# Threshold attention and a GELU MLP on one core: tail scores in two quarters of the array, joint transposes, and sums made earlier

## The chip, the cores and the metric

The kernel runs on one NeuronCore of a Trainium2 chip. Five engines work side by side, each through its own instructions in order, and wait for each other by semaphores: TensorE (PE in the profile, with PEld for the loads of its stationary operand), VectorE (DVE), ScalarE (ACT), GpSimd (POOL) and SyncE (SP, which here only issues transfers). Transfers between HBM and the on-chip memory (SBUF) are issued by SP, ACT and POOL and run on 16 DMA engines. PE writes its results into PSUM banks, from which DVE and ACT read.

The metric is the device time of one execution in microseconds (us). Ten runs of the kernel before gave a median of 1429.69 us, from 1428.52 to 1432.79.

## The reference

Inputs are `q`, `k`, `v` of shape (8 batches, 8 heads, 576, 64) in float32, a scalar `tau`, and two weights in float64, `w_in` (512 x 2048) and `w_out` (2048 x 512). For each head:

```
scores = q @ k.T / 8
scores = where(scores >= max(scores) - tau, scores, -1e9)      # per row
attn   = exp(scores - max(scores));  attn = attn / (sum(attn) + 1e-9)
out    = attn @ v
```

The heads are laid side by side into `x` (4608 tokens x 512), and the result is `gelu(x @ w_in) @ w_out` with the exact (erf) GELU, again 4608 x 512.

## The kernel before

**Attention.** Two heads, A and B (`e` = 0 and 1 in the code), are handled together as a pair: 64 channels each, so that the two fill 128 partitions. There are 32 pairs. The 576 queries of a pair are cut into four chunks of 128 (main slots, i = 0 to 3) and a rest of 64 (the tail slot, i = 4 = `NC`). The Python loop at the end of the kernel goes over the 160 slots `n` = (pair p, chunk i) and writes out, slot by slot, the order of instructions of each engine; nothing reorders them later.

In a slot, `scores` (L346) multiplies queries by keys. The 576 keys are done in two halves `h` of 288. In a main slot head A has its 64 channels in rows 0 to 63 of the array and head B in rows 64 to 127: four matmuls, each with 64 rows and 128 columns, into two PSUM tiles, one for each head. In a tail slot, both heads have 64 queries each. `q_tail` is a 128 x 128 tile that holds A's tail queries in its upper left and B's in its lower right quarter and zeros elsewhere (memsets on POOL, L102). Two matmuls over the whole array put A's scores into PSUM partitions 0 to 63 and B's into 64 to 127 of one tile. PSUM tiles of the tag `sc` have two buffers, taken in turn. In the profile each float32 matmul is two records.

`softmax_head` (L358) takes the negated row maximum on DVE (L367), the threshold on POOL (L368) and the exponential on ACT (L370). `softmax_tail` (L373) multiplies by the threshold's mask and sums, on DVE (L386); this is the last reader of the PSUM tile. For pairs 4 and later `turn_p` (L423) transposes the weights in 32 x 32 blocks on DVE, one operation for each head, B first, into `pd[0]` and `pd[1]` (or `pd_tail`), and `regroup` (L435) moves the blocks into place by transfers on SP, eight for two main slots. `weigh_v` (L450) multiplies by `v` two slots into the next pair, with matmuls of 128 rows and 64 columns, and DVE divides by the sums (L478), which have gone through HBM and back (`divisors`, L402).

The first four pairs (`EARLY`) are done in another way: PE transposes q, k (L275, L283) and the weights (L301, against a diagonal of the divisors made by ACT, L400, after a reciprocal on DVE, L397).

**Weights.** The float64 weights come in 32 pieces of 128 x 512, by two transfers each on POOL's queue (L154, L156), and are turned into float32 by bit operations: DVE (L176, L183, L185, L187) and ACT (L177). `conversions` is a generator; `convert(ns)` in the slot loop lets it advance by about `ns` of DVE time in each slot: 3000 in slots 0 to 7, 3650 after that, and all the rest at slot 19. Each finished piece calls `load_piece` for another. Odd pieces land in `pd`.

**MLP.** Blocks of 256 tokens. Blocks 0 to 9 go through two plain layers, L520 and L532, whose matmuls `fill` puts between the attention's, by a schedule of goals (`GOAL`, `PARTS`) in the slot loop. Blocks 10 to 17 are done after the attention, two at a time in four duos, by `strassen` (L607): seven products in place of eight on quarters of the operands. Its operands need sums: of `w_in` (`weights_in`, L581, called in the slot after the last attention slot, 12 operations; and L612 inside `strassen`), of the tokens (`x_sums`, L649, once for each duo) and of `w_out` (L658). Blocks 10 to 12 wait in HBM (`put_away`, `bring`) for lack of room. Results leave by rows of 512 (L537, L744, L749).

**Tables.** Exp and GELU need different tables in ACT; `table` (L504) reloads Exp's after each GELU by a small activation on the tile `warm`.

Of the kernel before, what the change touches and what calls it, by code (L numbers as in the profile page):

```python
# [18 lines left out]
def kernel(  # L19
# [69 lines left out]

    ident = const.tile([P, P], FP32, name="ident")  # L90
# [3 lines left out]
    q_tail = [const.tile([P, P], FP32, name=f"q_tail{i}") for i in range(4)]  # L94
    v_sb = [const.tile([P, 2, KR, D], FP32, name=f"v{i}") for i in range(4)]
    pd = [const.tile([P, 4 * KR, P], FP32, name=f"pd{e}") for e in range(2)]
# [4 lines left out]
    for t in q_tail + v_sb:  # L101
        nc.gpsimd.memset(t, 0.0)  # L102
# [156 lines left out]
    def turn_qk_early(p):  # L259
# [26 lines left out]
        for e in range(2):  # L286
            rows = slice(e * D, (e + 1) * D)
            nc.scalar.activation(
                qt[rows, e * TAIL:(e + 1) * TAIL], tr[rows, 0, 0:TAIL], AF.Copy, bias=0.0, scale=q_scale[rows])
# [36 lines left out]
    def turn_qk(p):  # L326

        s = st[p]
        qT = s["qT"] = ld.tile([P, MAIN], FP32, tag="qT", name="qT")
        kT = s["kT"] = ld.tile([P, S], FP32, tag="kT", name="kT")
        qt = s["q_tail"] = q_tail[p % 4]
        qs, ks = s.pop("q"), s.pop("k")
        nc.vector.transpose(kT.rearrange("p (b i) -> p b i", i=Q), ks)
        nc.scalar.activation(qs, qs, AF.Copy, bias=0.0, scale=q_scale)
        nc.vector.transpose(
            qT.rearrange("p (c a i) -> p c a i", c=NC, i=Q),
            qs[:, 0:MAIN // Q, :].rearrange("p (a c) j -> p c a j", c=NC))  # L340
        for e in range(2):
            rows = slice(e * D, (e + 1) * D)
            nc.vector.transpose(
                qt[rows, e * TAIL:(e + 1) * TAIL].rearrange("p (b i) -> p b i", i=Q), qs[rows, MAIN // Q:NB, :])

    def scores(p, i):  # L346
        s = st[p]
        n = 1 if i == NC else 2
        sc = s["sc", i] = [ps.tile([P, 2, 512], FP32, tag="sc", name="sc", bufs=2) for _ in range(n)]
        for h in range(2):  # L350
            for e in range(n):
                rows = slice(0, P) if i == NC else slice(e * D, (e + 1) * D)
                lhsT = s["q_tail"] if i == NC else s["qT"][rows, i * P:(i + 1) * P]
                at = h * HALF + (TAIL if p < EARLY and e == 0 else 0)
                nc.tensor.matmul(  # L355
                    sc[e][:, h, 0:HALF], lhsT=lhsT, rhs=s["kT"][rows, at:at + HALF], start=True, stop=True)
# [66 lines left out]
    def turn_p(p, i):  # L423
# [6 lines left out]
        n = 1 if i == NC else 2  # L430
        for e in reversed(range(n)):
            to = pd_tail[p % 2] if i == NC else pd[e][:, :, i * Q:(i + 1) * Q]
            nc.vector.transpose(to[:, 0:NB, :], w[:, e * S:(e + 1) * S].rearrange("p (b i) -> p b i", i=Q))  # L433
# [58 lines left out]
    warm = const.tile([P, 2], FP32, name="warm")  # L492
    nc.vector.memset(warm, 0.0)

# [15 lines left out]
    def block_steps(n):  # L510

        g = {}
        for j in range(N_DF):
# [11 lines left out]
        for m in range(TOK // P):  # L525
            for j in range(N_DF):
                yield NS_OUT, len(pieces) - N_DF + j + 1
# [11 lines left out]
    mlp = {"n": 0, "steps": None, "next": None, "debt": 0.0}  # L539
# [41 lines left out]
    def weights_in():  # L581
# [3 lines left out]
        rest = [units(v_sb[i % 4])[0] for i in range(NP - 4, NP - 1)]  # L585
# [9 lines left out]
        return (s1, s2, s4), room + rest  # L595
# [11 lines left out]
    def strassen(ext, room):  # L607
        s1, s2, s4 = ext
        for h in range(HF // U):
            for c in range(NK):  # L610
                a = w_in_sb[c][:, HF + h * U:HF + (h + 1) * U]
                vec.tensor_tensor(a, w_in_sb[c][:, h * U:(h + 1) * U], a, op=ALU.subtract)  # L612
        room = room + units(v_sb[(NP - 1) % 4]) + [u for t in pd_tail for u in units(t)]
        room += [x for _ in range(2) for x in unit(xg, "x", 2)]
        x_ext = [room.pop().rearrange("p (c t) -> p c t", c=NK) for _ in range(3)]
# [33 lines left out]
        def x_sums(n1, n2):  # L649
            t1, t2, t4 = x_ext  # L650
            a, b = x_blk[n1], x_blk[n2]
            b11, b21, b12, b22 = a[:, 0:NK, :], a[:, NK:2 * NK, :], b[:, 0:NK, :], b[:, NK:2 * NK, :]
            vec.tensor_tensor(t1, b12, b11, op=ALU.subtract)
            vec.tensor_tensor(t2, b22, t1, op=ALU.subtract)
            vec.tensor_tensor(b12, b22, b12, op=ALU.subtract)  # L655
            vec.tensor_tensor(t4, b21, t2, op=ALU.subtract)

# [7 lines left out]

        def finish_chunk(j, x, p3):
# [6 lines left out]
        x_sums(*DUOS[0])  # L673
        for sb, (n1, n2) in enumerate(DUOS):
# [45 lines left out]
            for m in ms:  # L720
# [3 lines left out]
                vec.tensor_tensor(lo[m][:, 0:HD], lo[m][:, 0:HD], vs[m], op=ALU.add)  # L724
            for n in DUOS[sb + 1] if sb + 1 < len(DUOS) else ():
                if n in away:
                    bring(n)
            if sb + 1 < len(DUOS):
                x_sums(*DUOS[sb + 1])
# [7 lines left out]
            for m in ms:  # L737
                product(ys[m], rows(g22, m, wt4))
                vec.tensor_tensor(hi[m][:, 0:HD], hi[m][:, 0:HD], ys[m], op=ALU.add)
            for m in ms:  # L740
                product(xs[m], rows(gs1, m, wt1))
                vec.tensor_tensor(hi[m][:, HD:2 * HD], hi[m][:, HD:2 * HD], xs[m], op=ALU.add)
                row = n2 * TOK + m * P
                nc.sync.dma_start(out[row:row + P, :], hi[m])  # L744
            for m in ms:
                product(xs[m], rows(g12, m, w_out_part(1, 1)))
                nc.scalar.copy(lo[m][:, HD:2 * HD], xs[m])
                row = n1 * TOK + m * P
                nc.sync.dma_start(out[row:row + P, :], lo[m])  # L749

    load_early(0)
    load_early(1)
# [32 lines left out]
    for n in range(len(slots) + WEIGH + 1):  # L785
# [60 lines left out]
        convert(3000 if n < 2 * HP else 3650 if n < BATCH - 1 else 1e9)  # L846
# [54 lines left out]
```

## Time and profile before

| | |
|---|---|
| Median of ten runs | 1429.69 us |
| The profiled execution | 1430.06 us, span 1427.9 us from its first to its last instruction |
| Granted TensorE clock, mean | 0.995 |
| Main-slot scores, L355 64\*128 64x288 | x960, 165.8 us busy, mean 435 ns |
| Tail-slot scores, L355 128\*128 128x288 | x120, 34.3 us busy, mean 408 ns |
| Transposes of the weights, L433 | x224 into `pd`, 160.7 us busy, mean 756 ns |
| Transposes of tail queries, L343 | x56, 12.2 us busy, mean 218 ns |
| HBM | 71.68 MB read, 11.47 MB written |

How to read the profile: a form such as 64\*128 64x288 gives the rows and columns of the array that a matmul uses and the shape of its moving operand. Matmuls are pipelined, so that the lengths of consecutive records overlap; the distance between two starts is what counts. "Idle before" is the time an engine stood still ahead of an instruction, with what ended it. The slices of the page cut the span into 40 parts of 35.7 us and give the busy share in tenths. All line numbers are those of the kernel before.

### The profile page before, as it was taken

How to read it: one execution, taken by the hardware profiler on the slowest of the kernel's cores; microseconds unless marked ns; L12 is line 12 of the kernel's file. 1: busy time of each engine (PE TensorE's matmuls, PEld its weight loads, DVE VectorE, ACT ScalarE, POOL GpSimd, SP SyncE). 2: the span in 40 equal slices, each digit the busy share in tenths (PEclk: the TensorE clock that was granted, in tenths of full speed). 3: DMA queues.
4: the chain of work that ended last, by engine and by line, in shares of the span. 5: the costliest groups of instructions: out<-in, count | busy, mean ns of one | idle time of the engine just before them, and what ended most of it. 6: DMA issues, size and time to landing. Idle time of an engine off the chain costs nothing.

```text
span 1427.9 us, 19776 instructions
## 1 busy us (share of the span) xinstructions
PE 1381.5 (97%) x6544; PEld 959.4 (67%) x6544; DVE 899.5 (63%) x1908; ACT 640.4 (45%) x1039; POOL 387.7 (27%) x810
## 2 busy tenths in 40 slices
PE   6898899999999999999999999999999999999999
PEld 4676447466465574655746657466488888888887
DVE  5887787877767777777777777777654142241330
ACT  5768525446255373562735627457142141230320
POOL 4443244443434434434334344330000000000000
PEclk9999999999999999999999999999999999999999
DMA  9978167776667776677766777765500100100000
GB/s 267 289 266 241 47 143 151 151 147 130 133 140 144 156 142 140 137 143 158 159 134 144 161 156 149 142 134 99 107 0 1 45 1 0 59 1 8 22 1 30
DMA packets 449492, 167.06 MB, mean 117 GB/s; under 512 B 413040, under 2 KB 432048, under 8 KB 449392
## 3 DMA queue, kind: packets, MB, share of 16 engines
q1 hardware_dynamic: 423184, 108.65, 39.1%
q0 software_dynamic: 23808, 56.57, 12.8%
q8 instruction: 53, 0.87, 0.3%
q10 hardware_dynamic: 2400, 0.59, 0.2%
q14 instruction: 47, 0.39, 0.1%
HBM read 71.68 MB, written 11.47 MB: 58 GB/s over the span
## 4 chain that ended last, share of the span: by engine, by line
PE 85%; DVE 6%; ACT 5%; DMA 2%; issue 1%; POOL 0%; SPq 0%; DVEq 0%; ACTq 0%; POOLq 0%
PE bank L641 27%; PE hT L520 18%; PE o_ps L532 18%; PE sc L355 12%; PE xT L460 10%; ACT p L370 2%; DVE p L386 2%; DVE nmx L367 1%; DMA raw<-in_moe_w_in_dram 1%; DVE power L185 1%; ACT L500 1%; PE tr L301 1%; ACT diag L400 1%; DMA pd<-in_moe_w_in_dram 1%; ACT L507 0%
## 5 line engine op out<-in xcount | busy, mean ns | idle before, releaser
L370 ACT ACTIVATE p<-sc,nmx 128x576 f32<-128x576 f32 x288 | 202.4, 739 | 384.1 <-DVE nmx L367 384.0
L367 DVE TENSOR_REDUCE nmx<-sc 128x1 f32<-128x576 f32 x288 | 204.8, 748 | 148.3 <-PE sc L355 148.3
L520 PE MATMUL hT<-x,w_in 128*128 128x256 f32 x1280 | 296.2, 384 | 0.0
L532 PE MATMUL o_ps<-w_out,g 128*128 128x512 f32 x640 | 294.2, 602 | 0.0
L520 PEld LDWEIGHTS hT<-x,w_in 128*128 128x128 f32 x1280 | 238.4, 190 | 56.9 <-issue 25.2
L386 DVE SCALAR_TENSOR_TENSOR p<-sc,thr,p 128x576 f32<-128x576 f32 x288 | 225.3, 816 | 65.5 <-ACT p L370 64.4
L368 POOL TENSOR_SCALAR thr<-nmx,tau_eff 128x1 f32<-128x1 f32 x288 | 84.6, 294 | 547.0 <-DVE nmx L367 544.5
L532 PEld LDWEIGHTS o_ps<-w_out,g 128*128 128x128 f32 x640 | 116.6, 190 | 140.3 <-issue 138.7
L355 PE MATMUL sc<-kT,qT 64*128 64x288 f32 x960 | 165.8, 435 | 2.6 <-DVE p L386 2.3
L460 PE MATMUL xT<-pT,v 128*64 128x288 f32 (+2 forms) x1280 | 164.1, 409 | 3.2 <-ACT g L500 3.2
L433 DVE STREAM_TRANSPOSE pd<-p 128x576 f32<-128x576 f32 x224 | 160.7, 756 | 2.9
L355 PEld LDWEIGHTS sc<-kT,qT 64*128 64x128 f32 x960 | 93.6, 188 | 84.3 <-issue 71.8
L460 PEld LDWEIGHTS xT<-pT,v 128*64 128x64 f32 x1280 | 90.6, 137 | 72.6 <-issue 13.2
L232 POOL DMA_DIRECT2D v<-in_v_dram x208 | 110.6, 534 | 10.4 <-issue 9.4
L641 PE MATMUL bank<-x,w_in 128*128 128x256 f32 x384 | 94.8, 383 | 3.2 <-DVE x L655 3.2
L507 ACT ACT_TABLE_LOAD x71 | 91.1, 1283 | 1.3
L500 ACT ACT_TABLE_LOAD x71 | 91.1, 1283 | 1.2
L641 PE MATMUL bank<-unit 128*128 128x256 f32 x352 | 88.6, 382 | 0.0
L641 PEld LDWEIGHTS bank<-x,w_in 128*128 128x128 f32 x384 | 73.7, 192 | 14.2 <-issue 4.1
L223 POOL DMA_DIRECT2D q<-in_q_dram x104 | 70.7, 685 | 15.6 <-issue 14.8
L301 PE MATMUL tr<-diag,p 128*128 128x128 f32 (+1 forms) x360 | 49.8, 302 | 25.0 <-ACT diag L400 16.0
L641 PEld LDWEIGHTS bank<-unit 128*128 128x128 f32 x352 | 67.5, 192 | 9.4
(143 smaller groups left out, 1342.1 us busy)
## 6 DMA issues: line engine op xcount, KB each, us to landing
pT<-pd SPq DMA_DIRECT2D x448, 160.0 KB, 3.9
pT<-pd_tail SPq DMA_DIRECT2D x112, 80.0 KB, 2.9
q<-in_q_dram POOLq DMA_DIRECT2D x104, 72.0 KB, 3.9
k<-in_k_dram POOLq DMA_DIRECT2D x104, 72.0 KB, 2.6
out_dram<-o_sb SPq DMA_DIRECT2D x28, 256.0 KB, 3.9
inv<-turned SPq DMA_DIRECT2D x56, 128.0 KB, 3.9
v<-in_v_dram POOLq DMA_DIRECT2D x156, 40.0 KB, 3.0
raw<-in_moe_w_in_dram POOLq DMA_DIRECT2D x8, 512.0 KB, 6.7
```

The lines of the kernel that those rows point to most:

```text
L232: eng.dma_start(t[r:P:4, e, 0:n, :], rows[:, r * KR:r * KR + n, :])
L355: nc.tensor.matmul(sc[e][:, h, 0:HALF], lhsT=lhsT, rhs=s["kT"][rows, at:at + HALF], start=True, stop=True)
L367: nc.vector.tensor_reduce(nmx[:, e:e + 1], sc, axis=AXIS.XY, op=ALU.max, negate=True)
L370: nc.scalar.activation(w[:, e * S:(e + 1) * S].rearrange("p (h s) -> p h s", h=2), sc, AF.Exp, bias=nmx[:, e:e + 1], scale=1.0)
L386: nc.vector.scalar_tensor_tensor(row, sc[e][:, :, 0:HALF], thr[:, e:e + 1], row, op0=ALU.is_ge, op1=ALU.mult, accum_out=den[e])
L433: nc.vector.transpose(to[:, 0:NB, :], w[:, e * S:(e + 1) * S].rearrange("p (b i) -> p b i", i=Q))
L460: nc.tensor.matmul(xT[f, 0:hi - lo], lhsT=s["v"][:, e, c, :], rhs=pT[:, c, lo:hi], start=(c == 0), stop=(c == KR - 1))
L500: nc.scalar.activation(t, hT, AF.Gelu)
L507: nc.scalar.activation(warm[:, 1:2], warm[:, 0:1], AF.Exp)
L520: nc.tensor.matmul(hT[:, j % 2, :], lhsT=w_in_sb[c][:, j * P:(j + 1) * P], rhs=x_blk[n][:, c, :], start=(c == 0), stop=(c == N_DM - 1))
L532: nc.tensor.matmul(o[:, 0:d_model], lhsT=g[j][:, m * P:(m + 1) * P], rhs=w_out_sb[j], start=(j == 0), stop=(j == N_DF - 1))
L641: nc.tensor.matmul(to, lhsT=l, rhs=r, start=start and k == 0, stop=k == len(pairs) - 1, skip_group_check=not start)
```

## The change

1. `q_tail` becomes 128 x 64: the queries of A in partitions 0 to 63, those of B in 64 to 127, without zeros and their memsets. The scores of a tail slot are four matmuls of 64 rows and 64 columns. Head A uses the upper left quarter of the array and head B the lower right one; while A does one half of the keys, B does the other, so that the two write different PSUM banks.
2. `q_tail` is filled by one operation in place of two (ACT in the early pairs, DVE in the others).
3. The two tiles `pd` become views of one tile, and `turn_p` transposes both heads by one operation.
4. The four updates of `w_in` (L612) and the first `x_sums` move from `strassen` into `weights_in`; their room comes from the tiles of `v`.
5. Strassen's results are stored by half rows, each half when it is done. One of these stores stands ahead of `bring` in SP's order.
6. The `warm` tile is set first, and Exp's table is loaded right after the first pair's loads are issued.
7. Conversions: `convert` advances by 0 in slot 0 and by 3400 in slots 1 to 7.

```diff
+    warm = const.tile([P, 2], FP32, name="warm")
+    nc.vector.memset(warm, 0.0)
...
-    q_tail = [const.tile([P, P], FP32, name=f"q_tail{i}") for i in range(4)]
+    q_tail = [const.tile([P, TAIL], FP32, name=f"q_tail{i}") for i in range(4)]
-    pd = [const.tile([P, 4 * KR, P], FP32, name=f"pd{e}") for e in range(2)]
+    turned_p = const.tile([P, 2, 4 * KR, P], FP32, name="turned_p")
+    pd = [turned_p[:, e, :, :] for e in range(2)]
-    for t in q_tail + v_sb:
+    for t in v_sb:
         nc.gpsimd.memset(t, 0.0)
...
+        nc.scalar.activation(qt, tr[:, 0, 0:TAIL], AF.Copy, bias=0.0, scale=q_scale)
...
+        nc.vector.transpose(qt.rearrange("p (b i) -> p b i", i=Q), qs[:, MAIN // Q:NB, :])
...
-        for h in range(2):
-            for e in range(n):
-                rows = slice(0, P) if i == NC else slice(e * D, (e + 1) * D)
-                lhsT = s["q_tail"] if i == NC else s["qT"][rows, i * P:(i + 1) * P]
-                at = h * HALF + (TAIL if p < EARLY and e == 0 else 0)
-                nc.tensor.matmul(
-                    sc[e][:, h, 0:HALF], lhsT=lhsT, rhs=s["kT"][rows, at:at + HALF], start=True, stop=True)
+        for k in range(2):
+            for e in range(2):
+                rows = slice(e * D, (e + 1) * D)
+                if i == NC:
+                    h = (k + e) % 2
+                    to, lhsT = sc[0][rows, h, 0:HALF], s["q_tail"][rows]
+                else:
+                    h = k
+                    to, lhsT = sc[e][:, h, 0:HALF], s["qT"][rows, i * P:(i + 1) * P]
+                at = h * HALF + (TAIL if p < EARLY and (e == 0 or i == NC) else 0)
+                nc.tensor.matmul(to, lhsT=lhsT, rhs=s["kT"][rows, at:at + HALF], start=True, stop=True)
...
-        for e in reversed(range(n)):
-            to = pd_tail[p % 2] if i == NC else pd[e][:, :, i * Q:(i + 1) * Q]
-            nc.vector.transpose(to[:, 0:NB, :], w[:, e * S:(e + 1) * S].rearrange("p (b i) -> p b i", i=Q))
+        if i == NC:
+            nc.vector.transpose(pd_tail[p % 2][:, 0:NB, :], w[:, 0:S].rearrange("p (b i) -> p b i", i=Q))
+            return
+        nc.vector.transpose(
+            turned_p[:, :, 0:NB, i * Q:(i + 1) * Q], w.rearrange("p (e b i) -> p e b i", e=2, i=Q))
...
-        rest = [units(v_sb[i % 4])[0] for i in range(NP - 4, NP - 1)]
+        x_ext = [units(v_sb[i % 4])[0].rearrange("p (c t) -> p c t", c=NK) for i in range(NP - 4, NP - 1)]
...
+        for h in range(HF // U):
+            for c in range(NK):
+                a = w_in_sb[c][:, HF + h * U:HF + (h + 1) * U]
+                vec.tensor_tensor(a, w_in_sb[c][:, h * U:(h + 1) * U], a, op=ALU.subtract)
+        x_sums(x_ext, *DUOS[0])
...
+        def store(n, m, t, at):
+            row = n * TOK + m * P
+            nc.sync.dma_start(out[row:row + P, at:at + HD], t[:, at:at + HD])
...
                 vec.tensor_tensor(lo[m][:, 0:HD], lo[m][:, 0:HD], vs[m], op=ALU.add)
+                store(n1, m, lo[m], 0)
...
     load_early(0)
+    nc.scalar.activation(warm[:, 1:2], warm[:, 0:1], AF.Exp)
     load_early(1)
...
-        convert(3000 if n < 2 * HP else 3650 if n < BATCH - 1 else 1e9)
+        convert(0 if n == 0 else 3400 if n < 2 * HP else 3650 if n < BATCH - 1 else 1e9)
```

## The prediction

> **What bounds the kernel now.** I read the page's busy table and slices first, then the timeline of PE around score slots, then the junction near 1030 us, then the first 40 us.
>
> ```profile
> PE 1381.5 (97%) x6544; PEld 959.4 (67%) x6544; DVE 899.5 (63%) x1908; ACT 640.4 (45%) x1039; POOL 387.7 (27%) x810
> PE   6898899999999999999999999999999999999999
> ```
>
> PE is busy 97% of the span. By windows it is busy 133.8 us of the first 166, 837.4 of the 843 us from 166 to 1009, 20.8 of the 24 us to 1033, and 389.5 of the last 395. So the first 166 us are bound by a chain through DVE, ACT and transfers; after that, whatever PE must do more is paid, and what other engines save is worth nothing unless PE waits for it.
>
> The timeline of PE (start, length, form, count, idle before) shows what score slots cost. A main slot is eight records in row halves (64\*128), a tail slot four records over the whole array (128\*128).
>
> ```profile
> 268.23 2.84 PE L532 MATMUL o_ps<-w_out,g 128*128 128x512 f32 x6
> 271.00 1.24 PE L355 MATMUL sc<-kT,qT 64*128 64x288 f32 x8
> 272.17 4.56 PE L532 MATMUL o_ps<-w_out,g 128*128 128x512 f32 x10
> 276.56 1.13 PE L355 MATMUL sc<-kT,q_tail 128*128 128x288 f32 x4
> 277.53 1.88 PE L532 MATMUL o_ps<-w_out,g 128*128 128x512 f32 x4
> 279.34 0.75 PE L355 MATMUL sc<-kT,qT 64*128 64x288 f32 x2
> 280.34 1.21 PE L355 MATMUL sc<-kT,qT 64*128 64x288 f32 x6 [0.25 <-DVE p L386]
> ```
>
> Starts count, since lengths overlap. The tail slot takes 277.53 - 276.56 = 0.97 us: 4 x 0.242, nothing lost at either side. A main slot streams the same 0.97 (eight records, two at once), but takes 1.17 from its start to the next product, and the products beside it lose time too: the x6 group takes 2.77 where six records 0.429 apart take 2.57. Record by record, an undisturbed main slot holds PE for 1.37 us, 0.40 more than a tail slot: 0.09 on entering the tiled form, 0.10 before its second pair, 0.10 on leaving, 0.10 before the second product after it. The value products, tiled by columns, show the same:
>
> ```profile
> 539.18 5.07 PE L460 MATMUL xT<-pT,v 128*64 128x288 f32 x40
> 544.18 2.84 PE L532 MATMUL o_ps<-w_out,g 128*128 128x512 f32 x6
> ```
>
> Twenty pairs at 0.242 are 4.85; they take 5.00. With entry and re-entry 0.09 + 0.05 + 0.10 + 0.10 = 0.34; here only 0.05 is lost before the second pair, for weight loads of 64 columns take 137 ns against 190.
>
> After each tail slot stands a wait. The next main slot's second matmul must take over the tail's PSUM buffer, held until DVE has finished with it:
>
> ```profile
> 277.74 0.76 DVE L367 TENSOR_REDUCE nmx<-sc 128x1 f32<-128x576 f32 x1 [0.79 <-PE sc L355]
> 279.37 0.82 DVE L386 SCALAR_TENSOR_TENSOR p<-sc,thr,p 128x576 f32<-128x576 f32 x1 [0.88 <-ACT p L370]
> ```
>
> So 279.34 starts with one head and its partner comes at 280.34. Against 1.37 us, the 27 main slots that follow a tail slot from 166 us on lose 0.52 us (14 of them), 0.87 to 1.66 (7) and 0.10 (6).
>
> The junction to the Strassen stage, and the start:
>
> ```profile
> 1028.12 1.03 PE L641 MATMUL bank<-x,w_in 128*128 128x256 f32 x4
> 1032.39 2.04 PE L641 MATMUL bank<-x,w_in 128*128 128x256 f32 x4 [3.24 <-DVE x L655]
> ```
>
> ```profile
> 1026.96 0.95 DVE L478 TENSOR_TENSOR x<-xT,inv 128x64 f32<-128x64 f32 x4 [5.05 <-DMA inv<-turned]
> 1027.83 2.48 DVE L612 TENSOR_TENSOR w_in<-w_in 128x512 f32<-128x512 f32 x4
> 1031.56 0.68 DVE L655 TENSOR_TENSOR x<-x 128x512 f32<-128x512 f32 x1
> ```
>
> ```profile
> 14.31 0.42 DVE L176 TENSOR_SCALAR expo<-raw 128x512 uint32<-128x512 uint32 x1
> ...
> 19.79 0.43 DVE L176 TENSOR_SCALAR expo<-raw 128x512 uint32<-128x512 uint32 x1 [2.00 <-DMA raw<-in_moe_w_in_dram]
> ...
> 20.54 1.40 DVE L367 TENSOR_REDUCE nmx<-sc 128x1 f32<-128x576 f32 x2
> 21.32 3.90 PE L301 MATMUL tr<-diag,p 128*128 128x128 f32 x20 [4.52 <-ACT diag L400]
> 24.76 0.61 POOL L154 DMA_DIRECT2D raw<-in_moe_w_in_dram  x1
> ...
> 33.87 0.43 DVE L176 TENSOR_SCALAR expo<-pd 128x512 uint32<-128x512 uint32 x1 [1.33 <-DMA pd<-in_moe_w_in_dram]
> ```
>
> **The change, part by part** (against the profiled execution, 1430.06 us: span 1427.9 and 2.2 around it; it stands 0.4 above the median, 1429.69).
>
> *Tail scores, steady part.* 28 slots from 166 us on. Four matmuls of 64x64 replace two of 128x128: eight records in pairs stream the same 0.97. No row shows quarters. Bounds: nothing (if they enter and leave like 128\*128), and 0.40 (row halves). I take 0.34, the column form, since quarters also load 64 columns: 28 x 0.34 = +9.6. Part comes back. The last score of the tail ends 0.14 later (entry 0.09, second pair 0.05), the next main slot starts 0.34 later, so its wait for the tail's buffer shrinks by 0.20: 21 x 0.20 + 6 x 0.10 = -4.8. Net +4.8; bounds 0 and 28 x 0.40 = +11.2 (nothing comes back).
>
> The Trainium skill weighs both ways here. "TensorE: Matmul & The Clock Gate", section "Measured speedup vs the span model", puts a pack of tiles at one matmul's duration and about 4 ns for each further tile; by it the tail slots would cost nothing and the whole sum would be 1428. "TensorEngine Tiling (Array Packing)", "Key Properties", says that a change of tiling mode drains the array, without a figure; the 0.40 of the main slots speaks for that one.
>
> *Tail scores, early part.* Four slots, 4 x 0.34 = 1.4 at most, 0 at least; PE is busy 80% there: +0.5.
>
> *A and B in one transpose, q_tail in one.* Two of 756 ns (1.44 us together) become one of 1152 elements: by 576 elements at 756 and 512 at 679, 1.2 ns an element, 1.35 to 1.45. Per pair a 218 ns transpose goes. All of it lies beside PE from 166 us on: 0. The transfers of head B, issued first, wait up to 0.7 us longer for the joint operation; they queue on SP one a microsecond and the pair is weighed two slots later (its products start 12 us after). If that cover went, 0.7 a pair, 20 us in all; no wait of a value product for these transfers is in the trace, so I charge 0.
>
> *Quarter sums earlier.* L612 and the four x_sums (2.48 + 2.7 us) go ahead of the last pair's divides. DVE ends the weight sums at 1021.9 and stands idle 5.05 us until the divisors land. The moved work ends near 1027.1, the divides still run at 1027.1 to 1028.0, and PE's second product at 1029.15 finds its sums made: -3.2 (bounds -3.24 and 0).
>
> *Stores in halves.* The last transfer is 128 KB, not 256: of its 2.0 us about 0.65 moved data, so -0.3 (0 to -0.65). Now a store stands on SP ahead of the fetch of each put-away block: the fetch moves from 1133 to about 1196, lands some 4 us later, and DVE's x_sums wait for it; after them DVE has 13.9 us free. Cost 0; if the cover went, at most 4 us.
>
> *Front.* ACT's table load (6.20 to 7.48) now runs before the input arrives: the first copy starts 7.49 with its transposes done 7.34, so -0.1. The loads of the second k go behind it on ACT, by 1 to 2 us, into the queue where the third needed 7.9 us; the transposes of the second k may come 1 us later. POOL's four memsets (0.63 us) go.
>
> *Conversion pacing.* At slot 0 none instead of 3000; slots 1 to 7 at 3400. 23,800 against 24,000: the same work. The second slot's maxima need not wait until 20.54: their scores (PE 14.28 to 16.8) let DVE begin near 16, a lead of up to 4.7 us. But DVE used that time for 3.5 us of conversions, which remain owed. And the loads of pieces 4 and 5, at 24.76 and 26.12 now, fall behind POOL's work of the third slot, near 29. DVE then reaches piece 4 at about 31 with 5 us of landing from 29: a stall of 2 to 3 us. By this working the fourth slot starts near 34.5 (now 34.28) with 2.2 us of conversions more to do. I take +1.5 for front and pacing together; bounds -4.7 (the lead stays) and +4.
>
> Sum: 1430.1 + 4.8 + 0.5 - 3.2 - 0.3 + 1.5 = 1433.4.
>
> **The rivals.** (1) *The early lead stays.* If DVE's later idle gaps (0.8 to 1.2 us at 36.50, 47.96, 50.58) take the owed conversions and no piece is late, the pacing gives -4.7: 1427.2, not slower. It decides once more than 1 us of the lead reaches 166 us. For it: PE waits 4.52 us there, its longest after the first load. Against: DVE is 88 to 95% busy from 50 to 100 us. (2) *Quarters switch free*: 1433.4 - 4.8 - 0.5 = 1428.1. Against it stand both tiled forms. (3) *The wait behind the tail does not shrink* (the other work of DVE or ACT sets it): 1433.4 + 4.8 = 1438.2. Against: DVE is idle 0.79 us before the tail's maximum. (4) *Quarters don't run two at once*: 4 x 0.242 more in 28 slots, 27.1: 1460.5. Row pairs and column pairs both do, so the diagonal should.
>
> **How the numbers follow.** The forecast has 0.50 (its own range 1431 to 1436.5), rival 1 0.18, rival 2 0.09, rival 3 0.15, rival 4 0.08. The range 1426 to 1440 leaves out rival 4 and the best ends of 1 and 2. Within 0.2%, about what a measurement tells from no change, is 1426.8 to 1432.6: half of 1, most of 2, some of the forecast, 0.26. Faster: rivals 1 and 2 together or a lead kept whole, 0.16. Slower 0.58.
>
> **What would show it.** Tail slots in 64\*64 form with about 1.3 us from start to the next product and a lost 0.1 after; main slots behind them losing about 0.3 and 0.75 instead of 0.5 and 0.95. No wait of PE for DVE x near 1029. The fourth slot's maxima near 34.5, with a DVE stall on a w_in piece just before. The forecast is wrong if quarters cost nothing at their edges, or if the chain up to 166 us moves by more than 3 us either way.

## The result, and the profile after

The changed kernel takes 1435.41 us (median of 14 runs, 1432.75 to 1438.3) beside 1429.78 us for the kernel before: ratio 1.0039, 95% interval 1.0031 to 1.0048, so 5.6 us slower. The prediction said 1433.4, slower. The profiled execution of the changed kernel took 1436.42 us, its span is 1434.6; against the profiled execution of before that is 6.7 us more span. From here on, an L number in a view is a line of the kernel that the view is of.

The page's busy table of the changed kernel (busy time, share of the span, instructions):

```profile
PE 1391.6 (97%) x6672; PEld 948.4 (66%) x6672; DVE 885.7 (62%) x1768; ACT 639.0 (45%) x1036; POOL 386.7 (27%) x806
```

VectorE (DVE) lost 13.8 us of work and TensorE (PE) gained 10.1 us. PE is still busy 97% of the span, so the first reading of before holds: what PE must do more is paid, and what DVE saves is not a gain by itself.

A tail slot and its neighbours in the timeline of PE after the change (start, length, form, count):

```profile
247.03 4.58 PE L520 MATMUL hT<-x,w_in 128*128 128x256 f32 x20
251.54 1.19 PE L357 MATMUL sc<-kT,q_tail 64*64 64x288 f32 x8
252.66 2.43 PE L520 MATMUL hT<-x,w_in 128*128 128x256 f32 x10
255.01 1.58 PE L357 MATMUL sc<-kT,qT 64*128 64x288 f32 x8
256.52 1.56 PE L520 MATMUL hT<-x,w_in 128*128 128x256 f32 x6
```

The form is 64\*64 and the eight records run two at once. From the tail's start to the next product are 1.12 us (252.66 - 251.54), where before they were 0.97; 0.10 more is lost on entering the tiled form and 0.10 before the second product behind it. Record by record the slot holds PE for 1.315 us in 27 of 28 cases, 0.345 more than before. The main slot behind the tail has lost most of its wait: it is one group of eight, with no pause after the second record. From its start to the next product it takes 1.51 us here, where an undisturbed one took 1.17.

The junction to the Strassen stage, in the timeline of PE after:

```profile
1037.94 3.70 PE L533 MATMUL o_ps<-w_out,g 128*128 128x512 f32 x8
1041.48 1.89 PE L653 MATMUL bank<-x,w_in 128*128 128x256 f32 x8
```

The first eight quarter products run without a pause. The 3.24 us wait of before is gone.

The first 35 us, in the timelines of PE and DVE:

```profile
14.96 1.09 PE L278 MATMUL tr<-ident,k 128*128 128x128 f32 x4 [2.50 <-DMA k<-in_k_dram]
```

```profile
18.52 1.42 DVE L368 TENSOR_REDUCE nmx<-sc 128x1 f32<-128x576 f32 x2 [3.67 <-PE sc L357]
...
34.51 0.43 DVE L179 TENSOR_SCALAR expo<-raw 128x512 uint32<-128x512 uint32 x1 [3.19 <-DMA raw<-in_moe_w_in_dram]
34.85 0.16 DVE L398 RECIPROCAL den<-den 128x2 f32<-128x2 f32 x1
34.93 1.40 DVE L368 TENSOR_REDUCE nmx<-sc 128x1 f32<-128x576 f32 x2
```

PE waits 2.50 us for the second k. The maxima of the second slot come at 18.52 (20.54 before), then DVE stalls 3.19 us on a piece of w_in, and the maxima of the fourth slot come at 34.93 (34.28 before). The early lead is spent by then.

The waits of DVE from 166 to 1030 us hold the surprise (total us, times, longest). Before, and after:

```profile
DVE x L478 <- DMA inv<-turned: 7.7, 5, 5.0
```

```profile
DVE x L480 <- DMA inv<-turned: 29.1, 16, 6.9
```

DVE waits 21 us longer for the divisors that `divisors` sends through DRAM (`turned` out, `inv` in); of the 7.7 us of before, 5.05 are the wait of the last divides at 1027 us, so up to there it is 2.6 against 29.1. Most of it is slack of DVE, but not all. The longest one in the timeline of after:

```profile
707.99 0.52 DVE L480 TENSOR_TENSOR x<-xT,inv 128x192 f32<-128x192 f32 x2 [6.87 <-DMA inv<-turned]
...
713.12 0.82 DVE L387 SCALAR_TENSOR_TENSOR p<-sc,thr,p 128x576 f32<-128x576 f32 x1 [0.21 <-ACT p L371]
```

```profile
714.10 1.38 PE L357 MATMUL sc<-kT,q_tail 64*64 64x288 f32 x8 [2.04 <-DVE p L387]
```

What DVE had queued behind the divides is late by as much, and PE stands 2.04 us for a score buffer.

Start times of the tail slots, compared between the two profiled executions, give the balance (after minus before, in us): +1.2 at 154, +4.5 at 188, +6.6 at 674, +10.6 at 735, +12.0 at 1009, +7.0 from the 200th record of the Strassen stage to the last. So: some 4.5 in the first 188 us, of which 1.2 stood at 154; 2.2 over 16 pairs from 188 to 674 and 1.3 over 9 pairs from 735 to 1009, 0.14 a pair; 4.0 in the two pairs around 705 to 735, where the divisors came late; -5.0 at the junction; and -0.3 between the last matmul and the end of the span. Between 154 and 188 us the clock is granted at half from 165.4 to 172.2 us, a loss of 3.4 us; before has no half clock between 72.2 and 1031.4 us. The divisors, this half clock and the size of the junction's gain were in no term of the prediction.

### The profile page after: what moved, and what is told of

Read it like the earlier page. It is cut to its first block, busy times and chain, and to the rows that moved or that the text cites. A ratio compares the mean times of both kernels' runs of the same rounds, so it can differ in the third digit from the quotient of the medians.

```text
span 1434.6 us, 19885 instructions
## 1 busy us (share of the span) xinstructions
PE 1391.6 (97%) x6672; PEld 948.4 (66%) x6672; DVE 885.7 (62%) x1768; ACT 639.0 (45%) x1036; POOL 386.7 (27%) x806
## 4 chain that ended last, share of the span: by engine, by line
PE 85%; DVE 6%; ACT 4%; DMA 3%; issue 1%; SPq 1%; POOL 0%; ACTq 0%; DVEq 0%; POOLq 0%
PE bank L653 27%; PE o_ps L533 19%; PE hT L520 17%; PE sc L357 12%; PE xT L462 9%; DVE p L387 2%; ACT p L371 1%; DVE power L188 1%; DMA k<-in_k_dram 1%; PE tr L301 1%; ACT diag L401 1%; DVE w_in L190 1%; DMA pT<-turned_p 1%; DVE nmx L368 1%; DMA turned<-turned 1%
## 5 line engine op out<-in xcount | busy, mean ns | idle before, releaser
L520 PE MATMUL hT<-x,w_in 128*128 128x256 f32 x1280 | 299.8, 387 | 0.0
L533 PE MATMUL o_ps<-w_out,g 128*128 128x512 f32 x640 | 297.3, 607 | 0.0
L357 PE MATMUL sc<-kT,qT 64*128 64x288 f32 x960 | 162.3, 433 | 1.0 <-DVE p L387 0.4
L434 DVE STREAM_TRANSPOSE turned_p<-p 128x1152 f32<-128x1152 f32 x112 | 154.1, 1376 | 3.0
L653 PE MATMUL bank<-w_out,unit 128*128 128x256 f32 x416 | 92.4, 379 | 0.0
L653 PEld LDWEIGHTS bank<-w_out,unit 128*128 128x128 f32 x416 | 79.0, 190 | 10.7
```

Of the source, the lines that this page charges most:

```text
L357: nc.tensor.matmul(to, lhsT=lhsT, rhs=s["kT"][rows, at:at + HALF], start=True, stop=True)
L434: nc.vector.transpose(turned_p[:, :, 0:NB, i * Q:(i + 1) * Q], w.rearrange("p (e b i) -> p e b i", e=2, i=Q))
L520: nc.tensor.matmul(hT[:, j % 2, :], lhsT=w_in_sb[c][:, j * P:(j + 1) * P], rhs=x_blk[n][:, c, :], start=(c == 0), stop=(c == N_DM - 1))
L533: nc.tensor.matmul(o[:, 0:d_model], lhsT=g[j][:, m * P:(m + 1) * P], rhs=w_out_sb[j], start=(j == 0), stop=(j == N_DF - 1))
L653: nc.tensor.matmul(to, lhsT=l, rhs=r, start=start and k == 0, stop=k == len(pairs) - 1, skip_group_check=not start)
```

## The experiments

All were compared with the kernel before on the same chip. "Unclear" below means that the interval holds 1. A difference in us is the ratio less one, times 1430, with the interval in brackets; where the medians are meant it says so.

| run | what it has | median us | ratio, 95% interval |
|---|---|---|---|
| e_junction | before + early quarter sums | 1425.01 | 0.9961 (0.9947 to 0.9976) |
| e_quarters | before + tails in quarters | 1431.84 | 1.0017 (1.0006 to 1.0027) |
| e_joint | before + joint transposes | 1428.91 | 0.9994 (0.998 to 1.0009) |
| e_front | before + moved table load | 1436.64 | 1.0047 (1.0029 to 1.0064) |
| e_front_late | same, behind both k | 1435.01 | 1.0035 (1.0021 to 1.0049) |
| e_pacing | before + spacing | 1431.49 | 1.0011 (0.9996 to 1.0026) |
| e_after_no_front | after - front | 1431.02 | 1.0007 (0.9992 to 1.0022) |
| e_junction_halves | before + sums + half stores | 1424.34 | 0.9962 (0.9947 to 0.9977) |
| e_shift | before, `warm` moved, the tiles behind it 32 bytes on | 1433.13 | 1.0024 (1.0013 to 1.0035) |
| e_after_unshifted | after, `warm` and its zeroing put back | 1433.66 | 1.0024 (1.0014 to 1.0034) |
| e_junction_halves_aligned | sums + half stores + 128 bytes | 1422.15 | 0.9946 (0.9933 to 0.996) |
| e_junction_halves_all_aligned | same + 160 more behind | 1424.29 | 0.9955 (0.9941 to 0.9968) |

### The parts alone

**The quarter sums.** The edit moves the `w_in` differences and the first four x_sums from the head of `strassen` to the end of what is yielded before it:

```diff
+        for h in range(HF // U):
+            for c in range(NK):
+                a = w_in_sb[c][:, HF + h * U:HF + (h + 1) * U]
+                vec.tensor_tensor(a, w_in_sb[c][:, h * U:(h + 1) * U], a, op=ALU.subtract)
+        x_sums(x_ext, *DUOS[0])
+        return (s1, s2, s4), x_ext, room
```

> The kernel before with part 4 alone: the updates of w_in and the first x_sums made in weights_in, ahead of the last divides. Theory: PE's wait of 3.24 us at the second Strassen product goes, and with it a stretch of half clock that follows the wait in the trace of before (granted clock 0.5 from 1030 to 1038.5 us, worth about 3 us): -6 us, 1423.5. Rival: only the wait goes, and the half clock comes from something else: -3.2 us, 1426.5.

Measured: 5.6 us faster (3.4 to 7.6; 4.5 at the medians), 1.7 times the 3.24 us of the wait. The reason stands in the granted clock. These are stretches of 10 us around the junction, first of before, then of this kernel (busy time and instructions of each engine, granted clock, DMA share, GB/s):

```profile
1023.00:1033.00 10.00, 6.76 (x27) 3.78 (x24) 5.85 (x12) 0.96 (x2) 0.00 (x0) 0.92 0.19 56
1033.00:1043.00 10.00, 10.00 (x36) 8.36 (x35) 2.83 (x8) 4.40 (x9) 0.00 (x0) 0.74 0.01 2
1043.00:1053.00 10.00, 10.00 (x48) 8.81 (x47) 6.79 (x18) 4.56 (x12) 0.00 (x0) 1.00 0.00 0
```

```profile
1025.00:1035.00 10.00, 10.00 (x45) 6.69 (x42) 5.21 (x12) 3.31 (x6) 0.00 (x0) 1.00 0.20 57
1035.00:1045.00 10.00, 10.00 (x48) 8.81 (x47) 6.25 (x17) 4.79 (x13) 0.00 (x0) 1.00 0.00 0
```

Behind the wait the clock of before is 0.74 over ten us, and PE, busy all the time, gets 36 products through where it gets 48 at full clock. The clock is granted at half from 1031.4 to 1038.2. Without the wait it stays at 1.00. So in this execution the wait cost its own 3.24 us and about half of 6.8 us behind it; between the two traces the junction gains 6.0 us.

That second part is not the same in every execution. In all traces the half clock comes in pieces of 3.41 us, or two or three of them in a row, at places that are a multiple of 3.41 us apart. Cutting a trace into windows at these places gives PE's work in each:

| wait of PE | PE busy in the windows that the wait touches, and in the next | half clock behind |
|---|---|---|
| before, 1032 us: 3.24 us | 1.18, 2.41, 3.41 us | 6.8 us, the second and third window |
| e_joint, 1032 us: 3.38 us | 2.25, 1.20, 3.41 us | 3.4 us, the third window |
| e_pacing, 1041 us: 3.27 us | 1.63, 1.93, 3.41 us | none |
| e_front_late, 1039 us: 3.42 us | 1.74, 1.66, 3.41 us | none |
| changed kernel, 714 us: 2.04 us | 1.37, 3.41 us | 3.4 us, the second window |
| e_junction, 826 us: 2.68 us | 1.81, 2.34, 3.32 us | none |

From 172 us to the last products, in all fourteen traces, half clock sets in after a window with at most 1.37 us of work and never after one with 1.63 us or more. (Up to 172 us, where PE mostly transposes, the border is less sharp: half clock sets in after windows with up to 2.2 us, and stays away after some with 1.6.) So it matters whether a wait falls into one window or across two. Seven traces have the wait at the junction, with 6.8 us of half clock behind it in three, 3.4 in two and none in two, 2 us lost at the mean: by this estimate the sums gain about 5.2 us, near the 5.6 measured. The Trainium skill ("TensorE: Matmul & The Clock Gate", "What's actually happening") describes half speed after an idle window of about 3.4 us, on a free-running window. The length and the fixed places agree with the traces; that the window has to be idle does not, for the one ahead of the half clock here held 1.18 us of work.

**The tails in quarters.**

```diff
+                if i == NC:
+                    h = (k + e) % 2
+                    to, lhsT = sc[0][rows, h, 0:HALF], s["q_tail"][rows]
```

> The kernel before with parts 1 and 2 alone: tail scores in quarters, q_tail filled by one operation. Theory: each of 28 tail slots holds PE 1.32 us in place of 0.97, and 0.19 of it comes back in the next main slot's wait: +5 us, 1434.8, main slots behind tails losing about 0.33 and 0.75 us. Rival A: nothing comes back, +9.6 us, 1439.4. Rival B: the loss in the changed kernel comes from the other parts, and this one alone is within 1 us of before.

Measured: 2.4 us slower, between the theory's value and nothing, its interval (0.9 to 3.9) just short of 5. The trace has the slope by itself: against the profiled execution of before this kernel stands at -2.6 us at the tail slot of 188 us and at +1.3 at the one of 1009, 3.9 us over 27 pairs, 0.146 a pair, 4.1 us for 28. The -2.6 at 188 us is not the edit's: e_junction stands at -1.9 there and e_joint at -2.3, both at about that since 78 us, ahead of anything that they change. The first 166 us differ by some 2 us from one profiled execution to the next.

**The joint transposes.**

```diff
+        nc.vector.transpose(
+            turned_p[:, :, 0:NB, i * Q:(i + 1) * Q], w.rearrange("p (e b i) -> p e b i", e=2, i=Q))
```

> The kernel before with part 3 alone: both heads transposed by one operation into one tile. Prediction's step: 0. Theory after the two traces: the transfers of a pair start about 0.6 us later each time on a queue (SP) that issues nearly all the time, the divisors land later, and DVE's waits for them grow (7.7 us in 5 waits before, 29.1 in 16 in the changed kernel); mostly hidden, 0 to +4 us where one of them reaches PE. Rival: the longer waits come from the quarters or the pacing, and here they stay at some 8 us.

Measured: no difference (-0.9 us, -2.9 to +1.3). In the changed kernel the 112 joint operations keep DVE busy for 154.1 us, where the 224 single ones took 160.7; no gain from the 6.6 us shows. DVE's waits for the divisors are 15.3 us in 12 here, twice those of before, as the theory had it; but two kernels below that have the joint operations too are at 4.8 and 5.6, so the operation alone does not lengthen them.

**The moved table load.** In this kernel `warm` is allocated and set to zero ahead of `ident`, as in the change, and ACT's first Exp stands between the loads of the two first pairs:

```diff
+    warm = const.tile([P, 2], FP32, name="warm")
+    nc.vector.memset(warm, 0.0)
     ident = const.tile([P, P], FP32, name="ident")
...
-    warm = const.tile([P, 2], FP32, name="warm")
-    nc.vector.memset(warm, 0.0)
...
     load_early(0)
+    nc.scalar.activation(warm[:, 1:2], warm[:, 0:1], AF.Exp)
     load_early(1)
```

> The kernel before with part 6 alone: Exp's table loaded behind the first loads. Theory: the second pair's k lands late and PE waits about 2.5 us for it near 15 us, as in the changed kernel, but the conversions of slot 0 hold the next slot's maxima until 20.5 anyway, so the time stays within 1 us of before. Rival: the late k reaches the end, +2.5 us.

Measured: 6.7 us slower, more than the whole change. Neither value was near. In the waits of PE of this kernel stand

```profile
PE sc L357 <- DVE p L388: 5.8, 11, 1.6
...
PE tr L277 <- DMA k<-in_k_dram: 3.2, 1, 3.2
```

The second k's first half goes out at 3.71 us instead of 2.53, its second half at 5.54 instead of 3.67. Now both transfers of the first piece of w_in (4.64 and 5.39) are issued ahead of it, and it lands at 15.65 instead of 7.63, behind the first transfer of the second piece as well (14.29). This was the first theory. But 2.3 us of waits for score buffers became 5.8 as well, late in the program (against before the kernel loses 1.8 to 188 us, nothing to 674, then 4.3 to 886), and no k is loaded there.

### Is it the late k?

The Exp is moved behind `load_early(1)`, the rest is kept as in e_front.

```diff
     load_early(0)
-    nc.scalar.activation(warm[:, 1:2], warm[:, 0:1], AF.Exp)
     load_early(1)
+    nc.scalar.activation(warm[:, 1:2], warm[:, 0:1], AF.Exp)
```

> Before, with the table loaded early, but behind the k transfers of both first pairs instead of between them. Theory (the table load itself is harmless; it held the second pair's k back on ScalarE's queue from 2.53 to 3.71 us, its second half then went out at 5.54, behind three transfers of the first piece of w_in, and landed at 15.65 instead of 7.63): the k lands at 7.6 again, PE no longer waits 3.2 us for it near 16, and the time is within 1 us of before. Rival (what cost 6.7 us when the front was moved alone is the early table or the warming itself, or the pieces that follow it): 5 us or more slower than before again.

The k went out at 2.53 and 3.62 and landed at 7.55, and PE did not wait for it. Yet the kernel is 5.0 us slower than before (3.0 to 7.0), as the rival had it. The theory fell: the late k is at most a small part. This run and e_front differ by it alone, 1.7 us, with intervals that overlap.

**The spacing alone.**

```diff
-        convert(3000 if n < 2 * HP else 3650 if n < BATCH - 1 else 1e9)
+        convert(0 if n == 0 else 3400 if n < 2 * HP else 3650 if n < BATCH - 1 else 1e9)
```

> Before with the new spacing of the conversions alone (first at once, then 3400 instead of 3000). Theory (the parts add up: junction -5.6, tails +2.4, joint transposes -0.6, front +6.7 give +2.9 of the +5.6 that the whole change costs, so the spacing has the rest): 2 to 3 us slower than before. Rival (the late k hides it or is what makes it bad): within 1 us of before. The prediction had front and spacing together at +1.5, between -4.7 and +4.

Measured: 1.6 us slower (-0.6 to +3.7; 1.3 at the medians), unclear between theory and rival.

**The changed kernel without the front.** `warm` is back in its place and the early Exp is gone (a diff against the changed kernel):

```diff
-    warm = const.tile([P, 2], FP32, name="warm")
-    nc.vector.memset(warm, 0.0)
     ident = const.tile([P, P], FP32, name="ident")
...
+    warm = const.tile([P, 2], FP32, name="warm")
+    nc.vector.memset(warm, 0.0)
...
-    nc.scalar.activation(warm[:, 1:2], warm[:, 0:1], AF.Exp)
     load_early(1)
```

> The changed kernel with the table loaded where it was before (no warming ahead of the second pair's k), all other parts kept. Theory (the late k costs the changed kernel what it cost alone): 6 us faster than the changed kernel, so about 1429, within 2 us of before. Rival (in the changed kernel the spacing sets the first slots anyway, so that the late k is hidden): still 1433 or more.

Measured: 1431.0, 4.4 us faster than the changed kernel at the medians, and within 2 us of before, as the theory has it. So the front costs the changed kernel most of what it loses. The trace speaks against the k as the cause: at 188 us this kernel stands at +4.1 us against before and the changed kernel at +4.5; the two part from 674 to 735 us (+6.3 to +6.6 here, +6.6 to +10.6 there). What is gone is the waits for the divisors, 5.6 us in place of 29.1.

**The quarter sums and the stores in halves.** Beside the edit of e_junction:

```diff
                 vec.tensor_tensor(lo[m][:, 0:HD], lo[m][:, 0:HD], vs[m], op=ALU.add)
+                store(n1, m, lo[m], 0)
...
                 vec.tensor_tensor(hi[m][:, 0:HD], hi[m][:, 0:HD], ys[m], op=ALU.add)
+                store(n2, m, hi[m], 0)
...
-                row = n2 * TOK + m * P
-                nc.sync.dma_start(out[row:row + P, :], hi[m])
+                store(n2, m, hi[m], HD)
```

> Before with the quarter sums behind the last slot and the stores in halves, nothing else. Theory (-5.6 for the sums as measured alone, -0.3 for the last store): about 1423.5. Rival (the additional stores share the queue with loads of the last products and cost more than they gain): 1425 or more.

Measured: 1424.34, about as e_junction's, so the half stores show nothing at the medians. In the trace they do: from the end of the last matmul to the end of the span it is 3.1 us here and in the changed kernel, 3.4 in e_junction and before.

### Is it the address?

What e_front and e_front_late share with the changed kernel, and no other kernel so far has, is the place of `warm`. Its 8 bytes take 32 in the allocation; ahead of `ident` they push all tiles from there to `w_out` 32 bytes on. In the built program `pd0` begins at byte 29312 of a partition before, 128 modulo 256, and at 29344 with `warm` in front, 160. The pieces that `regroup` fetches from pd are 256 bytes long, 512 apart. The times of transfers go with that: `pT<-pd` (`pT<-turned_p` where the two tiles are one) takes 4.12 to 4.14 us at the mean from issue to landing in the steady stage of the three kernels with the shift, 3.90 to 4.01 in all others so far. The test is one line, without any change of instructions:

```diff
+    warm = const.tile([P, 2], FP32, name="warm")
     ident = const.tile([P, P], FP32, name="ident")
...
-    warm = const.tile([P, 2], FP32, name="warm")
     nc.vector.memset(warm, 0.0)
```

> Before, with one line moved: the 8-byte tile warm is allocated ahead of ident instead of behind w_out, as in the changed kernel; no instruction is added, removed or moved. All tiles allocated between the two places (q_tail, v, pd, pd_tail, w_in, w_out) lie 32 bytes higher: pd at 160 instead of 128 modulo 256. Theory (what the moved front costs beyond the late k is this shift: the regrouping transfers pT<-pd take 4.12 to 4.14 us from issue to landing in the three kernels that have it, 3.91 to 4.01 in the seven without, and the divisors land late there): 4 to 5 us slower than before, transfers at 4.1. Rival (the addresses do nothing, the early table load itself does it): within 1 us of before, transfers at 3.9. The Trainium skill (DMA: Bandwidth & Descriptors, How a descriptor splits into AXI transactions) says that a piece that does not start at a multiple of 256 bytes is fetched from the boundary below; by its counting a 256-byte piece of pd would take 13 beats of 32 bytes instead of 12.

Measured: 3.4 us slower (1.9 to 5.0). The page's DMA queues (packets, MB, share of 16 engines' time) and DVE's wait for the divisors, of before and of this kernel:

```profile
q1 hardware_dynamic: 423184, 108.65, 39.1%
```

```profile
q1 hardware_dynamic: 423184, 108.65, 41.5%
```

```profile
DVE x L479 <- DMA inv<-turned: 18.6, 12, 4.9
```

The same packets with the same bytes take 6% more of the engines' time, `pT<-pd` takes 4.12 us, and VectorE waits 18.6 us for the divisors instead of 7.7. Against before this kernel loses 1.9 us to 188 us, nothing more to 674, and 3.4 from there to 917, where the longest of these waits lie (4.9 at 701 us, 4.4 at 793). That is the pattern of e_front. The part to 188 us is within what executions differ by. Waits for the divisors come without the shift as well, and one of 6.3 us in e_junction reaches PE; but up to 1020 us they add up to 2.3 to 9.6 us in the traces without the shift where pd is at 128 modulo 256, and to 16.4 to 33.1 in the four with it. All tiles between the two places move along; that it is pd whose place counts is read from the times of its transfers, no run moves pd alone.

The converse, a diff against the changed kernel: `warm` goes back to its place, and so does its zeroing; the early table load stays.

```diff
-    warm = const.tile([P, 2], FP32, name="warm")
-    nc.vector.memset(warm, 0.0)
     ident = const.tile([P, P], FP32, name="ident")
...
     dirty = [False]
+    warm = const.tile([P, 2], FP32, name="warm")
+    nc.vector.memset(warm, 0.0)
```

> The changed kernel, with the tile warm allocated where it was before, so that the table is still loaded early and the second k still goes out late, but no tile is shifted. Theory (the shift costs 4 to 5 us of the front's 6.7): 1430 to 1432, and the waits of VectorE for the divisors between 166 and 1030 us fall from 29 us to under 12. Rival (the early load itself costs it): 1435 as the changed kernel.

Measured: 1433.66. The time moved less than expected (-1.8, where -3.4 to -5.4 were expected; the intervals of the ratios, 1.0014 to 1.0034 and 1.0031 to 1.0048, touch), the waits moved as expected:

```profile
DVE x L478 <- DMA inv<-turned: 4.8, 6, 2.6
```

From 29.1 to 4.8 us. The 3.7 us that the changed kernel lost in the two pairs around 705 to 735 us are gone from this trace; in the Strassen stage it stands 3.2 us ahead of the changed kernel. Against e_after_no_front, which has no early load, it is 2.6 us slower at the medians. But this run makes the k later still: the early Exp waits for the zeroing of `warm`, which now comes at 4.21 us (0.81 in the changed kernel), the two halves go out at 4.85 and 5.44 instead of 3.63 and 5.42, and PE waits 3.82 us for them instead of 2.50. So the front's cost has two terms. The shift is shown: 3.4 us in e_shift, 1.8 at the medians here. What is left of the early load is not: with the k late or not (e_front, e_front_late) it is 6.7 and 5.0 us; with the early load or without it, and the k on time (e_front_late, e_shift), it is 5.0 and 3.4; both pairs of intervals overlap.

**Other addresses.** If 32 bytes cost time, the 128 that are left should too. The junction kernel with half stores gets 128 unused bytes in front and 128 behind, so that pd stands at 0 modulo 256 and the tiles behind `warm` stay as they were:

```diff
+    pad = const.tile([P, 32], FP32, name="pad")
     ident = const.tile([P, P], FP32, name="ident")
...
     warm = const.tile([P, 2], FP32, name="warm")
+    pad_end = const.tile([P, 32], FP32, name="pad_end")
```

> Before with the early quarter sums and the half stores, and with 128 unused bytes allocated ahead of ident and 128 behind warm: pd lies at 0 modulo 256 instead of 128, the tiles behind warm keep their places modulo 256. Theory (addresses set what the regrouping transfers take): pT<-pd falls below 3.8 us from 3.92, and the time by 0 to 3 us against 1424.3, since only 2 us of waits for the divisors are left there between 166 and 1030 us. Rival (only the odd 32 bytes matter, not the half of 256): transfers at 3.9, 1424 to 1425. The Trainium skill (the same section) would count 8 beats for a 256-byte piece of pd instead of 12.

Queue and issues (KB, median us to landing) of the unaligned kernel, then of this one:

```profile
q1 hardware_dynamic: 425488, 108.65, 39.3%
...
pT<-pd SPq DMA_DIRECT2D x448, 160.0 KB, 3.9
```

```profile
q1 hardware_dynamic: 425488, 108.65, 34.3%
...
pT<-pd SPq DMA_DIRECT2D x448, 160.0 KB, 3.7
```

The same packets take 13% less of the engines' time; the regrouping transfers go from 3.92 to 3.67 us at the mean, and no wait of DVE for divisors is left between 166 and 1030 us. The time is 1422.15, 2.2 us under the unaligned kernel at the medians, but the intervals overlap, and its profiled execution is no shorter (1419.3 against 1418.7, the shortest of that kernel's twelve): that the time gains is not shown.

The Trainium skill ("DMA: Bandwidth & Descriptors", "How a descriptor splits into AXI transactions") says that a piece that starts off a multiple of 256 bytes is fetched from the boundary below, the bytes ahead of it included. By its counting, an estimate, a piece of pd takes 13, 12 and 8 beats at 160, 128 and 0 modulo 256; the runs have the same order, 41.5, 39.1 and 34.3% of the engines' time, with smaller steps. The share also holds the queue's other transfers and the write side, which this counting leaves out.

The write side is the last run: 288 bytes behind `warm` instead of 128, so that pT and q, k, kT, p lie at 0 modulo 256 instead of 96 (x, raw, o_sb and others move as well).

```diff
-    pad_end = const.tile([P, 32], FP32, name="pad_end")
+    pad_end = const.tile([P, 72], FP32, name="pad_end")
```

> As the aligned kernel, with 288 instead of 128 unused bytes behind warm, so that pT, to which the regrouping transfers write, and q, k, kT, p move from 96 to 0 modulo 256 as well (x, raw, o_sb and the buffers of g from 224 to 128, turned from 224 and 96 to 128 and 0). Theory (the write side of a transfer pays for its address as the read side does): pT<-pd falls from 3.67 to about 3.4 us from issue to landing; the time stays within 1 us of 1422.2, because VectorE has no wait for the divisors left between 166 and 1030 us. Rival (only the side that is read pays): transfers at 3.67 again.

```profile
q1 hardware_dynamic: 425488, 108.65, 33.0%
...
pT<-pd SPq DMA_DIRECT2D x448, 160.0 KB, 3.4
```

The transfers fall to 3.46 us at the mean, as the theory had it, with the side that they read unchanged: the side that is written pays too. The time does not follow: 1424.29, 2.1 us at the medians above the kernel before it, where it was expected within 1 us; the intervals overlap. In the trace the difference is made before 190 us (2.9 us) and constant from there to the end. Where no one waits for the transfers in the steady stage, faster ones are worth nothing.

## Why the prediction was right, point by point

The time was right to 2 us, but two terms were wrong in opposite directions, the sums at the junction and the front. That their errors nearly cancel is luck.

- *Tail scores, steady part: right.* Predicted +9.6 of which 4.8 comes back; 0.34 a slot and 0.17 a pair. The slot costs 0.345, the net is 0.136 to 0.15 a pair, 4.1 us in e_quarters' trace. Main slots behind tails lose 0.34 us in 14 of 27 cases and 0.77 in five, as predicted (0.3 and 0.75). One detail was put badly: the "1.3 us from start to the next product" is the whole that the slot holds PE; from start to next product it is 1.12, the rest lies ahead of the first record and behind the next product. The rivals with free quarters, without the comeback and with quarters one after the other are out.
- *Tail scores, early part*: +0.5 is smaller than what executions differ by in the first 166 us; not settled.
- *Joint transposes: right at 0*, with an interval of -2.9 to +1.3. The operation takes 1376 ns (1350 to 1450 predicted).
- *Quarter sums: undersized.* Predicted -3.2 with -3.24 as the best bound; measured -5.6 (-7.6 to -3.4). The mechanism was right and the wait gone, but the sum took from the trace only the wait and not the half clock that followed it from 1031.4 to 1038.2. The clock was readable before the change: 0.74 in the ten us after the wait. What could not be read from one trace is that the half clock is there in only five of the seven profiled executions that have this wait.
- *Stores in halves: right at -0.3* in the trace; the time can't show it. The fetch behind the store goes out at 1203.5 us in the changed kernel and DVE waits 3.9 us for it, as worked out, and PE does not wait for that.
- *Front: wrong.* Predicted -0.1, with the second k 1 us later; alone it costs 6.7 us (4.1 to 9.1), in the changed kernel 4.4. The second k was late by 8 us, not one: 2 us in its issue put it behind large transfers of w_in. Whether that cost time is not shown. The larger error is what was not counted at all, where a tile stands: the prediction took the move of `warm` for a move of two instructions. The 32 bytes alone cost 3.4 us (1.9 to 5.0).
- *Conversion pacing: mechanism right, size open.* The maxima of the fourth slot came at 34.93 (34.5 predicted) behind a stall of 3.19 us on a piece of w_in (2 to 3 predicted), so the lead was gone as forecast and the rival in which it stays is out; in e_pacing, with the k on time, they come at 37.10 behind a stall of 4.41. Alone the spacing costs 1.6 us, with an interval of -0.6 to 3.7. The chain up to 166 us moved by 1.2 us at the tail slot of 154 us, within the 3 that the prediction allowed; the half clock from 165.4 us on comes on top.

Junction 2.4 us better than its term, tails some 1 to 3 better than theirs, front and pacing together up to 8.3 instead of 1.5: measured one by one, the parts add up to -5.6 + 2.4 - 0.9 + 6.7 + 1.6 = +4.2, each with an interval of 1.5 to 2.5 us to either side, and the whole costs 5.6.

## What to carry to other kernels

A line that only allocates is part of a change: list which tiles move when it moves, and where the staging tiles of many small transfers stand modulo 256. A wait of the bounding engine is worth more than its length when the granted clock behind it is below one, so read the clock of the ten us that follow before pricing its removal, and take the extra as a chance: in another execution the same wait may have none. A moved issue has to be priced by what gets ahead of it, not by its own delay.

## What the runs showed of the hardware that was not expected

- The same instructions, packets and bytes took 41.5%, 39.1% and 34.3% of the DMA engines' time with the source tile at 160, 128 and 0 modulo 256 bytes, and 33.0% with the destination at 0 too (the last two in the kernel with early sums and half stores, which has 39.3% without the padding).
- A wait of PE of 3.24 us was followed by 6.8 us at half clock; with it gone, the ten us have full clock and the time falls by 5.6 us. In other traces the same wait is followed by 3.4 us, or by none.
- A wait of 2.04 us of PE at 714 us in the changed kernel was followed by 3.4 us of half clock, while one of 2.68 us at 826.5 in e_junction was followed by full clock (1.00 from 830 to 835): length alone doesn't decide. What does go with it is PE's work in the 3.41 us window: 1.37 us in the first case, 1.81 and 2.34 in the two windows of the second.
